# Three moves in the opening of a fused attention and feed-forward kernel: an earlier request for a weight quarter, transposes ahead of table matmuls, one unit swapped in a hand-written order

## The chip, the cores and the metric

The kernel runs on one core of one Trainium2 chip. The metric is the device time of one execution in microseconds (us). Before the change three runs gave 323.81, 324.15 and 324.20 us, a median of 324.15.

The core has a matrix engine (TensorE, PE in the profile, with its weight loads shown as PEld), a vector engine (VectorE, DVE), a scalar engine (ScalarE, ACT), a general engine (GpSimd, POOL), a queue engine (SyncE, SP) and 16 DMA engines. Each compute engine works through its own instructions strictly in order and waits on semaphores for the others. DMA transfers are asked for by SP, ACT or POOL, and run by the 16 DMA engines.

## The reference

Sliding-window attention with a linear position bias per head, followed by a two-layer feed-forward part with a hard-swish between the layers:

```python
batch, n_heads, seq, head_dim = (8, 8, 576, 64)          # q, k, v in float32
scores = scale * q @ k.T;  rel = i - j
scores = where(0 <= rel < 128, scores - slope[h] * rel, -1e9)
attn = softmax(scores);  x = attn @ v                    # x: 4608 tokens x 512
h = x @ w_in                                             # 512 -> 2048
g = h * clip(h + 3, 0, 6) / 6
out = g @ w_out                                          # 2048 -> 512, float32
```

## The kernel before, in words

The order on all five engines is written out by hand: an instruction goes into its engine's stream in the order in which the program calls for it. Only waits on data and on free buffers come on top.

Attention goes by pairs of heads, g = 0 to 31, four pairs to a batch. For the first batch (pairs 0 to 3, `first_batch`, L558) q and k come as runs of nine tokens per partition. `prepare` (L208) casts a run to bf16, `transposes` (L219) turns q and then k with 18 small PE transposes each into a PSUM tile, and a copy (L220) brings each to qT and kT. `tables_diag` (L271) and `tables_off` (L307, L310) put the position bias into a PSUM bank by matmuls with the identity, and `scores_diag` (L296) and `scores_off` (L322, L328) add the score matmuls to it. `exp_full` takes the two exponentials of a pair on ACT (L348, L335), each of a tile of 128x1024. There are two such PSUM banks for scores, so a bank is free again once the exponential before last has read it.

`load_tokens` loads v of a batch as five blocks j of 128 tokens (the last of 64) through SP (L112). `cast_v(b, j, copy)` (L181) casts block j to bf16 into `vbuf`, on DVE (V) or POOL (P). `attend` multiplies the exponentials with v (L383, L391; the matmuls of the last block of queries, qt = 4, come last and are the only ones that read block 4) and divides by the sums on DVE (L412, L413). `back` transposes the result (L432) and copies it to xT (L434, L435, L438).

w_in comes in four quarters of 512 columns, asked for by POOL (`load_w_in`, L166): in `first_batch` the first stands between the casts of v, the second (`second_w_in`, L176) behind a one-element memset that waits for `attend(1)`, the others later. w_out follows in four parts (L171). q and k of the second batch are asked for by SP in `load_double` (L98), behind v; `prepare_double` (L227) casts them on POOL, and `wide_double` (L254) transposes them on PE.

The feed-forward part goes by nine chunks of 512 tokens. For each chunk 16 U units (`moe_up`: four matmuls L451 into a PSUM bank `hps`, then a relu on ACT, L470, and a product on DVE, L471, into `gbuf`) and 16 D units (`moe_down`: four matmuls L501 into a bank `ops`; four D units make 128 rows, then a copy L510 and a store). U units of chunk 1 on share two banks. `fill(n)` puts the next n units into the stream between steps of attention. Chunk 0's 16 U units come first; after that the strings in `ORDER` say how the U units of a chunk alternate with the D units of the chunk before. Their row for chunk 1 is taken in the segment for pairs 8 to 11, where `double` (L242) also transposes k and q with two tiles in turn, with one unit between the two.

In `first_batch`, PE's stream ends with `attend(3)`, `back(2)`, `up_begin(0, 0, 3)` (three of the four matmuls of the first U unit, which need w_in's first quarter and xT of pairs 0 to 2), `back(3)`, `wide_double(1, 0, "q")` and further units.

Of the kernel before, what the change touches and what calls it, by code (L numbers as in the profile page):

```python
# [18 lines left out]
def kernel(  # L19
# [76 lines left out]
    def load_double(b, dp, nm, eng):  # L96
        for e in range(2):
            eng.dma_start(out=ldbuf["qk".index(nm)][:, ds((2 * dp + e) * RT * D, RT * D)],  # L98
                          in_=src_of[nm][b, ds(4 * dp, 4), :, :].rearrange(
                              "(i e) (a t) d -> e a i (t d)", e=2, t=RT)[e])  # L100
# [7 lines left out]
    def load_tokens(b, nm):  # L108
        t = tokens(b, nm)
        for j in range(NQ):  # L110
            n = min(128, S - j * 128)
            nc.sync.dma_start(out=t[:n, j, :, :],  # L112
                              in_=src_of[nm][b, :, ds(j * 128, n), :].rearrange("h p d -> p h d"))
# [36 lines left out]
    def warm_up(n):  # L150
        w = ps_av.tile([128, 128], FP32, tag="av", name="w")
        for _ in range(n):
            nc.tensor.matmul(w, lhsT=ident, rhs=ident, start=True, stop=True)
# [11 lines left out]
    def load_w_in(g):  # L165
        nc.gpsimd.dma_start(  # L166
            out=w_in_sb[:, :, ts(g, 512)],
            in_=moe_w_in[:, ts(g, 512)].rearrange("(k p) f -> p k f", p=128))
# [6 lines left out]
    def second_w_in():  # L175
        nc.gpsimd.memset(w_out_sb[:, 4, 0:1], 0.0)  # L176
        load_w_in(1)

    def cast_v(b, j, copy):
        n = min(128, S - j * 128)  # L180
        copy(out=vbuf[b % 2][:n, j, :, 0:D], in_=ld[b, "v"][:n, j, :, :])  # L181
# [22 lines left out]
    def prepare(g, copies):  # L204
        for nm, copy in zip("qk", copies):
            pr = prs.tile([128, RT * D], BF16, tag=f"pr{nm}", name="pr",
                          padded_shape=[128, 2 * RT * D])
            copy(out=pr, in_=runs[nm][:, g % NP, :])  # L208
            st[g, nm] = pr

    def transposes(g, copies):
        b, hp = divmod(g, NP)
        for nm, dst, copy in (("q", qTb[b % 2], copies[0]), ("k", kTb[b % 2], copies[1])):
            src = st.pop((g, nm))
            tp = ps_h.tile([128, RT, RP], BF16, tag="h", name="tp", padded_shape=[128, 16, 64])
            for t in range(RT):
                for e in range(2):
                    r = slice(e * D, (e + 1) * D)
                    nc.tensor.transpose(tp[r, t, :], src[r, ts(t, D)], ident[r, r])  # L219
            copy(out=dst[:, hp, :, :].rearrange("p j c -> p (j c)")[:, 0:S].rearrange(  # L220
                "p (a t) -> p a t", t=RT), in_=tp.rearrange("p t a -> p a t"))
# [38 lines left out]
    def full(g):  # L260
        return g < NB_FULL * NP
# [4 lines left out]
    def tables_diag(g):  # L266
        scd = ps_sc.tile([128, 2, 512], FP32, tag="sc", name="scd")
        st[g, "scd"] = scd
        for e in range(2 if diag_tabled(g) else 0):
            t = tab[:, 2 * (g % NP) + e, 1:2, :]  # L270
            nc.tensor.matmul(scd[:, e, :].rearrange("p (j c) -> p j c", j=4), lhsT=ident,  # L271
                             rhs=t.to_broadcast([128, 4, 128]), start=True, stop=False)
# [12 lines left out]
    def scores_diag(g):  # L285
        rooms(g)
        b, hp = divmod(g, NP)
        qT, kT = qTb[b % 2][:, hp, :, :], kTb[b % 2][:, hp, :, :]
        first = not diag_tabled(g)
        if (g, "scd") not in st:  # L290
            tables_diag(g)
        scd = st[g, "scd"]
        for j in range(4):
            for e in range(2):
                r = slice(e * D, (e + 1) * D)
                nc.tensor.matmul(scd[:, e, ts(j, 128)], lhsT=kT[r, j, :],  # L296
                                 rhs=qT[r, j, :], start=first, stop=first or j == 3)

    def tables_off(g):
        hp = g % NP  # L300
        sco = ps_sc.tile([128, 2, 512], FP32, tag="sc", name="sco")
        st[g, "sco"] = sco
        if full(g):
            for e in range(2):
                h = 2 * hp + e
                t = tab[:, h, 0:1, :]
                nc.tensor.matmul(sco[:, e, 128:512].rearrange("p (j c) -> p j c", j=3),  # L307
                                 lhsT=ident, rhs=t.to_broadcast([128, 3, 128]),
                                 start=True, stop=False)
                nc.tensor.matmul(sco[:, e, 0:128].rearrange("p (s c) -> p s c", s=2),  # L310
                                 lhsT=ident, rhs=tab[:, h, :, 0:64], start=False, stop=False)

    def scores_off(g):
        b, hp = divmod(g, NP)
        qT, kT = qTb[b % 2][:, hp, :, :], kTb[b % 2][:, hp, :, :]
        foff = not full(g)
        if (g, "sco") not in st:
            tables_off(g)
        sco = st[g, "sco"]
        for e in range(2):  # L320
            r = slice(e * D, (e + 1) * D)
            nc.tensor.matmul(sco[:, e, 64:128], lhsT=kT[r, 4, :],  # L322
                             rhs=qT[r, 4, 0:LAST], start=foff, stop=foff)
        for j in range(4):
            n = 128 if j < 3 else LAST
            for e in range(2):
                r = slice(e * D, (e + 1) * D)
                nc.tensor.matmul(sco[:, e, ds((j + 1) % 4 * 128, n)], lhsT=kT[r, j, :],  # L328
                                 rhs=qT[r, j + 1, 0:n], start=foff, stop=foff or j == 3)
# [8 lines left out]
    def exp_full(g):  # L338
        for e in range(2):
            exp_diag(g, e)  # L340
        exp_off_full(g)
# [113 lines left out]
    def up_begin(nt, ms, n):  # L455
        hps = ps_h.tile([128, NT], FP32, tag="h", name="hps")
        up_mms(nt, ms, 0, n, hps)
        begun[nt, ms] = hps, n
# [29 lines left out]
    def moe_down(nt, step):  # L488
# [14 lines left out]
        if part == 3:  # L503
# [5 lines left out]
            else:  # L509
                nc.vector.tensor_copy(out=osb, in_=ops[nt, sub])  # L510
                nc.sync.dma_start(out=out[rows, :], in_=osb)

    ORDER = [("UUDUDUUDUD", "UUDUDUDUD", "UDUDUDD", "UUDDDD"),
             ("DDDD", "UUDUDUDUD", "UUDUDUDUD", "UUDUDUDDUU"),
             ("DDDD",) * 4]
    units = [(0, moe_up, step) for step in range(16)]
    for nt in range(1, n_nt + 1):
        ups, downs = iter(range(16)), iter(range(16))
        for c in "".join(ORDER[0 if nt == 1 else 2 if nt == n_nt else 1]):
            units.append((nt, moe_up, next(ups)) if c == "U" else (nt, moe_down, next(downs)))  # L520
# [12 lines left out]
    V, P, A = nc.vector.tensor_copy, nc.gpsimd.tensor_copy, nc.scalar.copy  # L533
# [24 lines left out]
    def first_batch():  # L558
        prepare(0, (V, A))
        warm_up(20)  # L560
        tables_diag(0)
        tables_off(0)
        warm_up(10)
        transposes(0, (V, A))
        scores_diag(0)
        prepare(1, (P, V))
        transposes(1, (V, V))
        scores_off(0)
        exp_full(0)
        scores_diag(1)  # L570
        prepare(2, (P, P))
        tables_off(1)
        transposes(2, (V, V))
        scores_off(1)
        exp_full(1)
        scores_diag(2)
        prepare(3, (P, V))
        tables_off(2)
        transposes(3, (V, V))
        scores_off(2)  # L580
        exp_full(2)
        scores_diag(3)
        scores_off(3)
        exp_full(3)
        cast_v(0, 0, V)
        cast_v(0, 1, P)
        load_w_in(0)
        cast_v(0, 2, V)
        cast_v(0, 3, V)
        cast_v(0, 4, P)  # L590
        for dp in range(2):
            for nm in "kq":
                load_double(1, dp, nm, nc.sync)
        load_tokens(1, "v")
        attend(0)
        attend(1)
        back(0)
        attend(2)
        back(1)
        second_w_in()  # L600
        prepare_double(1, 0, (P, P))
        attend(3)
        back(2)
        up_begin(0, 0, 3)
        back(3)
        wide_double(1, 0, "q", V)
        prepare_double(1, 1, (P,), "k")
        load_w_in(2)
        prepare_double(1, 1, (P,), "q")
        load_w_in(3)  # L610
        for dp in range(2):
            for nm in "kq":
                load_double(2, dp, nm, nc.sync)
        up_begin(0, 1, 3)
        done[0] = NP
        fill(1)
        wide_double(1, 0, "k", A)
        fill(2)
# [147 lines left out]
```

## Time and profile before

| what | value |
|---|---|
| runs, us | 323.81, 324.15, 324.20 |
| the profiled execution, its own time, us | 323.38 |
| its span, us | 321.7 |
| instructions | 7010 |
| busy share of the span | PE 96%, ACT 61%, DVE 54%, POOL 44% |
| DMA in the span | 51.90 MB, mean 161 GB/s |
| granted TensorE clock | 1.00 |

The span reaches from the first to the last instruction of the profiled execution. Times inside it count from the span's start. A row of a timeline reads: start, length, engine, line, operation, what it writes and reads, and in square brackets the idle time of its engine just before it and what ended that. A row of the chain of waits reads: start, length, and the work or the wait. A transfer has a row where it is asked for (the queue of the asking engine: SPq, POOLq); the time until it has landed is given with the DMA issues.

### The profile page before, as it was taken

Reading aid. Unit: us, or ns where it says so; the run is one execution under the profiler, and the core shown is the slowest. Engines: PE = TensorE matmul, PEld = TensorE weight load, DVE = VectorE, ACT = ScalarE, POOL = GpSimd, SP = SyncE. Lnnn points to the kernel's source line nnn. Section 1 sums busy time; section 2 is a strip of 40 time slices with the busy share of each in tenths; the row PEclk is TensorE's granted clock in tenths of the full one; section 3 lists DMA queues with packets and bytes.
Section 4 is the critical chain, followed back from the end, with each engine's and each line's share of the span. In section 5 each row is a group of like instructions: output and inputs, shape, how many; then the busy total and the mean of one; then the engine's idle time right before and its main releaser. Section 6 shows DMA issues by size and latency. Waiting matters only on the chain.

```text
span 321.7 us, 7010 instructions
## 1 busy us (share of the span) xinstructions
PE 308.1 (96%) x2699; PEld 166.7 (52%) x2738; DVE 172.7 (54%) x338; ACT 195.1 (61%) x334; POOL 140.7 (44%) x249
## 2 busy tenths in 40 slices
PE   6879999999999999999999999999999999999996
PEld 5465465555555455455677644554554444444443
DVE  6657675554356555555555556555655455455510
ACT  4748976877777766666676657666764344244401
POOL 8456592683494767356745664563331000000000
PEclk9999999999999999999999999999999999999999
DMA  7999999899999999999999999932112200000112
GB/s 277 202 319 225 272 255 208 223 235 204 220 223 184 220 198 201 200 223 205 186 191 191 229 176 201 211 108 86 23 53 64 76 34 35 33 33 33 67 52 79
DMA packets 131425, 51.90 MB, mean 161 GB/s; under 512 B 118976, under 2 KB 123328, under 8 KB 131392
## 3 DMA queue, kind: packets, MB, share of 16 engines
q1 hardware_dynamic: 126160, 45.36, 67.0%
q0 software_dynamic: 4224, 4.19, 8.3%
q10 hardware_dynamic: 1008, 1.90, 1.6%
q8 instruction: 21, 0.34, 0.5%
q14 instruction: 12, 0.10, 0.1%
HBM read 36.70 MB, written 9.44 MB: 143 GB/s over the span
## 4 chain that ended last, share of the span: by engine, by line
PE 82%; DMA 5%; ACT 4%; POOL 4%; issue 2%; DVE 2%; SPq 1%; POOLq 0%
PE ops L501 35%; PE hps L451 35%; DMA ldbuf<-in_q_dram 3%; PE scd L296 2%; DMA qTb<-tbuf 2%; PE av L391 2%; PE av L383 2%; ACT r L470 2%; PE sco L328 1%; PE ops L482 1%; ACT kTb L244 1%; PE tp L254 1%; POOL tbuf L194 1%; ACT gbuf L351 1%; SPq L98 1%
## 5 line engine op out<-in xcount | busy, mean ns | idle before, releaser
L471 DVE SCALAR_TENSOR_TENSOR gbuf<-r,hps 128x512 bf16<-128x512 f32 x144 | 98.7, 687 | 102.5 <-ACT r L470 100.2
L470 ACT ACTIVATE r<-hps,bias 128x512 f32<-128x512 f32 x144 | 98.9, 689 | 89.5 <-PE hps L451 88.2
L451 PE MATMUL hps<-xT,w_in_sb 128*128 128x512 bf16 (+1 forms) x621 | 142.7, 358 | 2.3 <-DMA w_in_sb<-in_moe_w_in_dram 0.9
L501 PE MATMUL ops<-w_out_sb,gbuf 128*128 128x512 bf16 x540 | 134.2, 380 | 2.3 <-issue 1.7
L451 PEld LDWEIGHTS <-w_in_sb 128*128 128x128 bf16 x640 | 58.8, 98 | 54.8 <-DMA w_in_sb<-in_moe_w_in_dram 1.3
L501 PEld LDWEIGHTS <-gbuf 128*128 128x128 bf16 x560 | 52.2, 98 | 57.2
L354 POOL TENSOR_SCALAR_AFFINE_SELECT pd<-pd 128x512 bf16<-128x512 bf16 x48 | 29.6, 631 | 34.5 <-ACT pd L351 34.4
L364 POOL TENSOR_SCALAR_AFFINE_SELECT po<-po 128x512 bf16<-128x512 bf16 x48 | 30.1, 633 | 32.7 <-ACT po L361 32.6
L351 ACT ACTIVATE pd<-scd,bias_d 128x512 bf16<-128x512 f32 x48 | 31.6, 685 | 5.0 <-PE scd L296 3.6
L194 POOL CAST tbuf<-ldbuf 128x512 bf16<-128x512 f32 (+1 forms) x45 | 25.5, 611 | 18.7 <-DMA qTb<-tbuf 9.8
L510 DVE COPY osb<-ops 128x512 f32<-128x512 f32 x33 | 22.7, 687 | 20.3 <-PE ops L501 20.3
L361 ACT ACTIVATE po<-sco,bias_o 128x512 bf16<-128x512 f32 x48 | 33.1, 689 | 0.0
L402 DVE TENSOR_TENSOR avs<-av,rc 128x384 bf16<-128x384 f32 (+1 forms) x48 | 23.6, 491 | 1.6
L391 PEld LDWEIGHTS <-pd 128*128 128x128 bf16 x192 | 14.4, 97 | 8.3 <-issue 0.5
L383 PE MATMUL av<-vbuf,po 128*128 128x65 bf16 x192 | 18.1, 193 | 0.1
L391 PE MATMUL av<-vbuf,pd 128*128 128x65 bf16 x192 | 17.5, 194 | 0.3 <-ACT kTb L244 0.3
L383 PEld LDWEIGHTS <-po 128*128 128x128 bf16 x192 | 14.4, 98 | 3.1 <-DVE avs L402 0.5
L187 POOL CAST vbuf<-ldbuf 128x1024 bf16<-128x1024 f32 x14 | 14.3, 1040 | 3.2 <-DMA ldbuf<-in_v_dram 3.2
L367 ACT ACTIVATE p4buf<-sco,bias_d 128x64 bf16<-128x64 f32 x48 | 15.5, 324 | 0.0
L227 POOL CAST pr<-ldbuf 128x576 bf16<-128x576 f32 x20 | 12.8, 669 | 4.4 <-DMA ldbuf<-in_k_dram 3.4
L296 PE MATMUL scd<-qTb,kTb 64*128 64x128 bf16 x256 | 12.7, 219 | 1.8 <-DVE kTb L220 1.1
L296 PEld LDWEIGHTS <-kTb 64*128 64x128 bf16 x256 | 7.2, 94 | 13.5 <-issue 9.7
(96 smaller groups left out, 215.0 us busy)
## 6 DMA issues: line engine op xcount, KB each, us to landing
out_dram<-osb SPq DMA_DIRECT2D x33, 256.0 KB, 2.4
ldbuf<-in_v_dram SPq DMA_DIRECT2D x32, 256.0 KB, 5.3
ldbuf<-in_q_dram SPq DMA_DIRECT2D x20, 256.0 KB, 5.1
ldbuf<-in_k_dram SPq DMA_DIRECT2D x16, 256.0 KB, 4.6
ldbuf<-in_q_dram SPq DMA_DIRECT2D x12, 288.0 KB, 6.4
ldbuf<-in_k_dram SPq DMA_DIRECT2D x12, 288.0 KB, 6.4
w_in_sb<-in_moe_w_in_dram POOLq DMA_DIRECT2D x4, 512.0 KB, 9.2
w_out_sb<-in_moe_w_out_dram POOLq DMA_DIRECT2D x4, 512.0 KB, 11.1
```

The lines of the kernel that those rows point to most:

```text
L194: nc.gpsimd.tensor_copy(out=tbuf[:m, :, j, :], in_=s[:m, j, :, :].rearrange("p (i e) d -> p i (e d)", e=2))
L296: nc.tensor.matmul(scd[:, e, ts(j, 128)], lhsT=kT[r, j, :], rhs=qT[r, j, :], start=first, stop=first or j == 3)
L351: nc.scalar.activation(out=pd[:, e, :, :].rearrange("p j c -> p (j c)"), in_=sc[:, e, :], func=ACT.Exp, bias=bias_d[:, h:h + 1], scale=scale)
L354: nc.gpsimd.affine_select(out=pd[:, e, :, :], in_=pd[:, e, :, :], pattern=[[0, 4], [1, 128]], channel_multiplier=-1, base=0, compare_op=AL ...
L361: nc.scalar.activation(out=po[:, e, :, :].rearrange("p j c -> p (j c)"), in_=sc[:, e, :], func=ACT.Exp, bias=bias_o[:, h:h + 1], scale=scale)
L364: nc.gpsimd.affine_select(out=po[:, e, :, :], in_=po[:, e, :, :], pattern=[[0, 4], [-1, 128]], channel_multiplier=1, base=-1, compare_op=A ...
L383: nc.tensor.matmul(out_av, lhsT=po[:, e, qt % 4, :], rhs=vb[:, qt - 1, h, :], start=True, stop=False)
L391: nc.tensor.matmul(out_av, lhsT=d, rhs=vb[:, qt, h, :], start=(qt == 0), stop=True)
L451: nc.tensor.matmul(hps[:, lo:hi], lhsT=w_in_sb[:, ks, ts(ms, 128)], rhs=xT[:, ks, ds(src, hi - lo)], start=(ks == 0), stop=(ks == n_ks - 1))
L470: nc.scalar.activation(out=r6, in_=hps, func=ACT.Relu, bias=bias3[:, 0:1], scale=1.0 / 6.0)
L471: nc.vector.scalar_tensor_tensor(out=gts[nt][:, ms, :], in0=r6, scalar=1.0, in1=hps, op0=ALU.min, op1=ALU.mult)
L501: nc.tensor.matmul(ops[nt, sub], lhsT=gts[nt][:, ms, ts(sub, 128)], rhs=w_out_sb[:, ms, :], start=(ms == 0), stop=(ms == n_ms - 1))
```

## The change: what it does

Three edits:

1. In `first_batch`, `transposes` of pairs 2 and 3 stands before `tables_off` of pairs 1 and 2 instead of behind it. The instructions are the same.
2. The first quarter of w_in is asked for behind the cast of v's block 0, which goes to POOL; block 1's cast goes from POOL to DVE. Before, it was asked for behind block 1's cast on POOL.
3. The order of units for chunk 1: the tenth unit becomes a U and the D that stood there comes after it, so that one more U is ahead of chunk 0's later downs; the last row has one U less. There are 16 of each as before.

```diff
-    ORDER = [("UUDUDUUDUD", "UUDUDUDUD", "UDUDUDD", "UUDDDD"),
+    ORDER = [("UUDUDUUDUUD", "UUDUDUDUD", "UDUDUDD", "UDDDD"),
              ("DDDD", "UUDUDUDUD", "UUDUDUDUD", "UUDUDUDDUU"),
              ("DDDD",) * 4]
...
         prepare(2, (P, P))
+        transposes(2, (V, V))
         tables_off(1)
-        transposes(2, (V, V))
         scores_off(1)
         exp_full(1)
         scores_diag(2)
         prepare(3, (P, V))
+        transposes(3, (V, V))
         tables_off(2)
-        transposes(3, (V, V))
         scores_off(2)
         exp_full(2)
         scores_diag(3)
         scores_off(3)
         exp_full(3)
-        cast_v(0, 0, V)
-        cast_v(0, 1, P)
+        cast_v(0, 0, P)
         load_w_in(0)
+        cast_v(0, 1, V)
         cast_v(0, 2, V)
         cast_v(0, 3, V)
         cast_v(0, 4, P)
```

## The prediction

> **What bounds the kernel now.** The page first: TensorE (PE) is the bound, and it is short of work only at the start.
>
> ```profile
> PE 308.1 (96%) x2699; PEld 166.7 (52%) x2738; DVE 172.7 (54%) x338; ACT 195.1 (61%) x334; POOL 140.7 (44%) x249
> PE   6879999999999999999999999999999999999996
> DMA  7999999899999999999999999932112200000112
> ```
>
> Each digit is a slice of 8.04 us. PE is at 6, 8 and 7 tenths in the first three slices, then full until the last. By windows it idles 2.49, 1.10 and 2.21 us in 0:8, 8:16 and 16:24, together 5.8 us, and then some 0.4 us per 8 us. So whatever makes PE's stream start earlier or later near 24 us moves the end one for one, as long as nothing stalls it afterwards. Next the chain of waits in order of time, cut to where PE's idling ends:
>
> ```profile
> 14.50 8.26 DMA ldbuf<-in_q_dram
> 22.76 0.05 issue
> 22.81 0.68 POOL pr L227
> 23.49 0.05 issue
> 23.54 0.68 PE tp L254 x9
> ```
>
> PE starts its full stretch at 23.54, with L254 of the q of batch 1, pairs 0 and 1. That waited for POOL's cast, and the cast for a q load landing at 22.76. A second chain arrives just ahead of it (timelines of PE and POOL):
>
> ```profile
> 16.76 0.23 PE L391 MATMUL wide<-vbuf,w_out_sb 128*128 128x65 bf16 x2 [0.24 <-ACT w_out_sb L348]
> 22.37 0.60 PE L451 MATMUL hps<-xT,w_in_sb 128*128 128x512 bf16 x2 [0.94 <-DMA w_in_sb<-in_moe_w_in_dram]
> 22.80 0.44 PE L432 MATMUL tb<-ident,avs 128*128 128x128 bf16 x5
> ...
> 11.82 0.62 POOL L181 CAST vbuf<-ldbuf 128x512 bf16<-128x512 f32 x1 [1.69 <-DMA ldbuf<-in_v_dram]
> 12.38 0.88 POOL L166 DMA_DIRECT2D w_in_sb<-in_moe_w_in_dram  x1
> 15.80 0.87 POOL L181 CAST vbuf<-ldbuf 64x512 bf16<-64x512 f32 x1 [2.54 <-DMA ldbuf<-in_v_dram]
> 17.97 0.74 POOL L166 DMA_DIRECT2D w_in_sb<-in_moe_w_in_dram  x1
> ```
>
> The reader is to see two things. `attend(0)` starts at 16.76, when the exponentials let it, and v's last block is cast on POOL at 15.80 to 16.67: both release it within 0.1 us. And PE waits 0.94 us for the first w_in quarter, but L254 would wait until 23.54 in any case.
>
> **Part 1, transposes ahead of tables** (pairs 2, 3). Nothing is added; the four table matmuls (9.85 to 10.39, 0.54 us) go behind the 36 transposes. `scores_off` comes no sooner, but DVE's copies start 0.54 earlier (10.91 becomes 10.37), so kT of pair 2 is ready at 11.8 and ScalarE (ACT) loses its gap of 0.28 before 12.83; the same happens for pair 3. ACT's gaps before 12.83, 14.39 and 15.69 are 0.28, 0.54 and 0.28: the gain is between 0 and 1.1. Followed through in order I get 0.8: the last exponential ends near 16.8 instead of 17.63, and `attend(0)` could begin near 15.9. This pays only if v is there.
>
> **Part 2, w_in earlier.** The three v casts that change hands cost nothing: DVE's three casts of 0.42 us and POOL's of 0.62 have idle time around them. What counts is the DMA issue. Block 0 of v was issued at 4.62 and lands some 6.1 us later (the two issues in 4.6:5.05 have a median of 6.4, the second alone 6.7), so near 10.7; POOL has been free since 10.13. Its cast ends at 11.3 and the quarter is asked for at 11.28 instead of 12.38, 1.1 us earlier. In the queue rows its first packets come in 13:14 (3 packets), so they would come near 12.9. Now what is then in the DMA engines:
>
> ```profile
> q8 instruction: 1, 0.02, 4.5%
> ...
> q1 hardware_dynamic: 568, 0.14, 67.6%
> q0 software_dynamic: 3, 0.00, 2.0%
> ...
> q0 software_dynamic: 29, 0.03, 57.3%
> q1 hardware_dynamic: 77, 0.04, 26.4%
> ...
> q0 software_dynamic: 176, 0.18, 106.8%
> q1 hardware_dynamic: 83, 0.02, 16.0%
> ```
>
> (queue: packets, MB, share of 16 engines; windows 10.25:12, 13:14, 14:15 and 34:35.) An instruction fetch held one engine for 4.5% of 16 x 1.75 us, 1.26 us, in the midst of v. So v's packets are nearly all through by 14, and a tail of about 70 small ones trickles on to 15, as slowly as one engine moves them; block 4 lands at 15.8 for that engine's sake. Before, w_in came at 14.0 and needed about 0.9 us to get into stride (29 packets in 14:15 against 176 in a full us), so it missed v. Now it is in stride at 13.8, with 60 to 70 packets of v left on the late engine. The last pair of rows shows what happens when both are there: quarter 3 of w_in beside v of batch 1, where 256 B packets get no more than one turn per 1 KB packet. Those v blocks (issued 28.41 and 29.26) took 9.5 us each to land, those of batch 0 took 5.5 to 7.7.
>
> The price. A quarter is 512 packets, 32 per engine, at 106.8% x 16 / 176 = 0.097 us: 3.1 us. Turn about, the v tail is held by at most that, and by nothing if w_in again comes too late on that engine: 0 to 3.1 us. I take 3.1, because more than 32 packets are left; block 4 lands near 18.9. The Trainium skill, "DMA: Bandwidth & Descriptors", section "Queues, rings and completion order", says that an engine goes round its queues by whole packets of some 9 to 17 descriptors. By that, taking the rows' packets for its descriptors and four of 1 KB to a turn of w_in, 65 small ones would need about five turns of 0.39 us, an estimated 2 us instead of 3.1; the rows of 34:35 speak for one to one.
>
> Behind it: POOL's cast of block 4 (0.61 to 0.87) ends near 19.6, the last four value matmuls of `attend(0)` near 19.9, and its reciprocal starts at 19.8 to 20.0 instead of 17.51, 2.3 late. From there four attends and backs run at their own pace (reciprocals at 17.51, 18.51, 19.68, 20.94), so `back(2)`'s transposes go from 20.99 to 23.3 and xT of pair 2 from 22.11 to 24.4. w_in is then long there (0.94 saved); the three matmuls of `up_begin` and `back(3)` end at 24.9 to 25.0, and L254 goes from 23.54 to about 24.95: **+1.4**. Queued behind v's cast on POOL is also `second_w_in`: asked for near 20.3 instead of 17.97, its packets come near 21.8, against 22 before (q0 falls to 7 packets in 21:22 and stands at 78 in 22:23: the next quarter starts when the one before has landed). So q's last load gets at most 0.4 us of extra turns: it lands at 22.8 to 23.7, its cast ends by 24.4, and it no longer decides. The casts of k for pairs 2 and 3 (25.80 now) may come near 27.1, L254 on them wants 26.52 + 1.4 = 27.9: covered. w_in's second quarter (needed at 28.35 now, landed at 17.97 + 10.4 = 28.4) would land near 28.4 and be needed at 29.8: covered.
>
> **Part 3, the order.** One U moves ahead of the fourth D, and the two kinds alternate one place shifted until the string's last rows. Sixteen of each remain. Loss: the U that now comes at 58.73 needs the bank of the U two before, whose product DVE ends at 58.28 + 0.69 = 58.97: 0.27 late. Gain: in two pairs (before 72.44 and 80.66) a D instead of a U stands between the two transposes of `double`, so ACT's second copy needn't wait behind a relu, and the waits of 0.17 each go. Bounds -0.4 to +0.3; I take **-0.1**. The last part of w_out (issued at 42.9, landing 13.6 us or less later) is wanted 0.86 later than now, which costs nothing.
>
> **Sum.** +1.4 - 0.1 = +1.3. The profiled execution took 323.38 us (span 321.7 and 1.68 around it), so 324.7 for it; it lies 0.77 under the median of the runs, 324.15, to which the forecast is given: **325.4 us**. Its own range, with v's delay between 2 and 3.1 and the extra turns of w_in against q, is 324.9 to 326.2.
>
> **Rivals.**
> Faster: w_in fills the gap. In 14:15 the engines moved only 65 GB/s, against 391 in 19:22; packets brought into that us let k and q land up to 0.8 us earlier, and if v slips by less than 0.5 us, part 1 is worth its 0.8 at the attends. Then L254 starts near 22.7, -0.8, with part 3 -0.9: 323.25. It decides if the late engine has fewer than five packets of v left when w_in is in stride. For it: the idle us and PE's 0.94 wait. Against: the tail of 77 packets, and that q's late packets share an engine that is busy throughout.
> No change: w_in is served on the late engine only behind v, as before. Then quarter 0 and q land there as before, L254 stays at 23.54, and 324.05 follows from part 3 alone. For it: before, the tail of v kept its pace after 14 although w_in had begun elsewhere. Against: 1.1 us more of v are still to come.
> That the change doesn't ask earlier at all would need block 0 to land after 11.8; it is issued 0.4 us before block 1, which landed then, so this gets no chance of its own.
>
> **Chances.** Forecast (slower) 0.55, faster 0.25, no change 0.20. With 0.2% (0.65 us, what a measurement of this kernel can tell): faster 0.25, same 0.20, slower 0.55. The range reaches from the faster case to the top of the forecast's own: 323.1 to 326.2.
>
> **What would show it.** Right: POOL's wait for v's block 4 ends near 18.9 rather than 15.8; PE's `attend(0)` stands split before its last matmuls; L254 starts near 25 and is released by L432 or xT, not by q; w_in's first quarter lands before 19 and no PE wait on it is left. Wrong: block 4 at 15.8 to 16.3 and L254 at or before 23.5. Part 3 is wrong if the two waits of 0.17 stay or if L451 waits more than 0.3 near 59.

## The result, and the profile after

| | runs | median, us | lowest to highest |
|---|---|---|---|
| before, beside the change | 15 | 323.24 | 322.8 to 324.3 |
| the change | 15 | 325.04 | 324.2 to 325.4 |

The ratio of the two is 1.0044, with a 95% interval of 1.0032 to 1.0055: 1.4 us slower, clear of noise and clear of the 0.2% (the two medians lie 1.8 us apart). The profiled execution of the change took 324.83 us (span 323.1), that of before 323.38 (span 321.7): 1.45 us apart. In the wider set of runs the kernel before has a median 0.9 us lower than in the three shown ahead of the prediction.

The page of the change, for the rows shown of before:

```profile
PE 309.9 (96%) x2699; PEld 168.6 (52%) x2738; DVE 172.3 (53%) x338; ACT 194.8 (60%) x334; POOL 140.1 (43%) x249
PE   7879999999999999999999999999999999999996
PEclk9979999999999999999999999999999999999999
```

The loss stays within the opening, and a new thing stands there: the granted TensorE clock falls in the third slice, where before it was at 9 throughout. The chain of waits, in order of time (start, length, what), says what the opening waits for:

```profile
10.23 7.98 DMA ldbuf<-in_v_dram
18.21 0.06 issue
18.27 0.61 POOL vbuf L181
18.89 0.04 issue
18.93 0.19 PE wide L391
...
24.48 0.38 PE hps L451
24.86 0.28 PE tb L432 x5
25.13 0.50 PE tp L254 x9
```

(A row of the chain starts where the work ahead of it ends; in the timeline L254 starts at 24.97.) Before, this chain came to L254 through a load of q. Now it comes through v: the last block, asked for at 10.23, takes 7.98 us to land (5.5 before), and L254 follows on the attends with no wait for q. The timelines of POOL, PE and DVE show the links:

```profile
11.18 0.88 POOL L166 DMA_DIRECT2D w_in_sb<-in_moe_w_in_dram  x1
18.27 0.60 POOL L181 CAST vbuf<-ldbuf 64x512 bf16<-64x512 f32 x1 [6.20 <-DMA ldbuf<-in_v_dram]
...
18.93 0.19 PE L391 MATMUL wide<-vbuf,w_out_sb 128*128 128x65 bf16 x1 [1.66 <-POOL vbuf L181]
...
19.26 0.22 DVE L412 RECIPROCAL rcw<-wide 128x10 f32<-128x10 f32 x1 [3.73 <-PE wide L391]
22.14 0.22 DVE L412 RECIPROCAL rcw<-wide 128x10 f32<-128x10 f32 x1 [0.81 <-PE wide L391]
...
24.97 0.67 PE L254 MATMUL tp<-ident,pr 128*128 128x128 bf16 x9
```

The first and the third reciprocal of before:

```profile
17.51 0.22 DVE L412 RECIPROCAL rcw<-wide 128x10 f32<-128x10 f32 x1 [1.31 <-PE wide L391]
19.68 0.22 DVE L412 RECIPROCAL rcw<-wide 128x10 f32<-128x10 f32 x1
```

w_in is asked for 1.2 us earlier than before (12.38); v's block 4 is cast 2.5 us later (15.80); PE stands still for 1.66 us in the middle of `attend(0)`; DVE's first reciprocal is 1.75 us late (17.51), its third 2.46 us (19.68); L254 starts at 24.97 instead of 23.54, 1.43 us late. The queue rows (packets, MB, share of 16 engines) of the windows 13:14, 14:15 and 15:16 show what holds v:

```profile
q0 software_dynamic: 72, 0.07, 69.4%
q1 hardware_dynamic: 180, 0.04, 26.3%
...
q0 software_dynamic: 179, 0.18, 115.2%
q1 hardware_dynamic: 26, 0.01, 3.8%
...
q0 software_dynamic: 147, 0.15, 88.8%
q1 hardware_dynamic: 123, 0.03, 23.5%
```

In 14:15, where SP's queue was down to 77 packets before, w_in (q0) has 179 packets, as many as in the 34:35 of before (176), and v (q1) has 26. In 15:16 they share, about one for one.

### The profile page after: what moved, and what is told of

It is laid out like the page before. It is cut to its first block, busy times and chain, and to the rows that moved or that the text cites. A ratio compares the mean times of both kernels' runs of the same rounds, so it can differ in the third digit from the quotient of the medians.

```text
span 323.1 us, 7012 instructions
## 1 busy us (share of the span) xinstructions
PE 309.9 (96%) x2699; PEld 168.6 (52%) x2738; DVE 172.3 (53%) x338; ACT 194.8 (60%) x334; POOL 140.1 (43%) x249
## 4 chain that ended last, share of the span: by engine, by line
PE 81%; DMA 6%; ACT 4%; issue 2%; DVE 2%; POOL 2%; SPq 1%; ACTq 0%; POOLq 0%; DVEq 0%
PE ops L501 35%; PE hps L451 35%; DMA ldbuf<-in_v_dram 2%; PE scd L296 2%; DMA qTb<-tbuf 2%; PE av L391 2%; ACT r L470 2%; PE av L383 2%; DMA ldbuf<-in_k_dram 2%; PE sco L328 1%; SPq L112 1%; PE ops L482 1%; PE tb L432 1%; ACT xT L438 1%; DVE gbuf L471 1%
## 5 line engine op out<-in xcount | busy, mean ns | idle before, releaser
L510 DVE COPY osb<-ops 128x512 f32<-128x512 f32 x33 | 22.7, 687 | 22.0 <-PE ops L501 21.9
## 6 DMA issues: line engine op xcount, KB each, us to landing
w_out_sb<-in_moe_w_out_dram POOLq DMA_DIRECT2D x4, 512.0 KB, 12.3
```

## The experiments

Every kernel ran beside the kernel before on the same chip; the ratio is to that.

| kernel | runs | median, us | before, us | ratio, 95% interval |
|---|---|---|---|---|
| part2_alone | 12 | 324.70 | 323.34 | 1.0027, 1.0009 to 1.0045 |
| parts13 | 12 | 324.00 | 323.34 | 1.0013, 0.9999 to 1.0028 |
| part1_alone | 12 | 323.23 | 323.34 | 0.9996, 0.9974 to 1.0018 |
| part3_alone | 12 | 323.65 | 323.34 | 1.0007, 0.9993 to 1.0021 |
| keep_pe_busy | 12 | 324.35 | 323.38 | 1.0024, 1.0009 to 1.0039 |
| casts_only | 12 | 323.26 | 323.38 | 0.9992, 0.9974 to 1.0010 |
| two_quarters | 6 | 327.19 | 323.38 | 1.0097, 1.0070 to 1.0125 |
| try_better | 12 | 322.95 | 323.38 | 0.9983, 0.9967 to 0.9999 |
| block3_last | 10 | 322.65 | 323.39 | 0.9979, 0.9960 to 0.9999 |
| best_of_parts | 12 | 322.75 | 323.39 | 0.9981, 0.9965 to 0.9997 |
| block3_last_earlier | 12 | 323.10 | 323.26 | 0.9984, 0.9963 to 1.0004 |
| best_order | 12 | 323.12 | 323.26 | 0.9984, 0.9963 to 1.0005 |

The medians of any one kernel are blurred by about 1 us that has nothing to do with the opening. In the profile of part1_alone, for one, the stretch from 107 to 125 us is 1.5 us longer than in that of before: POOL waits 6.2 us for a DMA transpose (`qTb<-tbuf`) instead of 4.8, and PE then waits 1.1 us for POOL's masks. So the readings below rest on the place of the steps in the profiles first, and on the medians second.

### Each part alone

**part2_alone**: the kernel before with

```diff
-        cast_v(0, 0, V)
-        cast_v(0, 1, P)
+        cast_v(0, 0, P)
         load_w_in(0)
+        cast_v(0, 1, V)
```

> The kernel before with the w_in request behind block 0's cast, and nothing else. If w_in holding v's block 4 is the cause, this alone costs the whole: block 4 lands near 18.3 instead of 15.8, DVE's first reciprocal of attend starts near 19.3, L254 near 25.0 instead of 23.5, and the time is 1.2 to 1.6 us over before (ratio 1.004 to 1.005). If the order of units or the transposes bring the loss, the ratio is under 1.002.

**parts13**: the change with these lines undone, the rest kept.

> The change without the w_in part. If w_in holding v's block 4 is the cause, block 4 lands near 15.8 again, L254 starts at 23.0 to 23.6 and the time is within 0.4 us of before (ratio 0.999 to 1.001), at best 0.5 faster, since w_in's first quarter and q still land near 22. If the cause is the order of units (its late bank near 59) or the transposes, the ratio stays near 1.004.

**part1_alone** and **part3_alone**: the kernel before with the two `transposes` moved, and with the new first row of `ORDER`.

> Only the transposes ahead of the tables. ACT's last exponential of the first batch ends 0.7 to 0.9 us sooner (near 16.9 instead of 17.6), but v's block 4 (cast until 16.7) and w_in and q (landing near 22 and 22.8) stay, so the time moves by 0 to -0.3 us. Rival: the opening is paced by ACT, then -0.7.

> Only the order of units for chunk 1. My sum had -0.1 us: two waits of 0.17 us of PE on ACT's copy L244 (before 72.4 and 80.7) go, and one wait on DVE's product near 59 to 66 comes. Rival: the waits only move, and the time is the same within 0.1 us, or +0.3 if the bank is late more than once.

POOL's cast of v's last block in part2_alone, and in parts13:

```profile
18.43 0.61 POOL L181 CAST vbuf<-ldbuf 64x512 bf16<-64x512 f32 x1 [6.25 <-DMA ldbuf<-in_v_dram]
```

```profile
15.68 0.61 POOL L181 CAST vbuf<-ldbuf 64x512 bf16<-64x512 f32 x1 [2.40 <-DMA ldbuf<-in_v_dram]
```

With part 2 block 4 is held, without it it is not; L254 starts at 25.57 in part2_alone and at 23.66 in parts13, where POOL's cast of q releases it as before. By the medians part 2 alone is 1.4 us slower, by the ratio 0.3 to 1.5, so this agrees with the whole loss without pinning it; the ratio itself is below the 1.004 that was expected. L254 is 0.6 us later than in the change, and the clock of this profile is at 0.50 for 6.83 us instead of 3.41. Five of its 12 runs kept a clock of 1.00; their median is 323.94, that of the other seven 325.03. parts13 lies 0.4 us above before by the ratio, with an interval from no loss to 0.9 us; in its profile w_in's second quarter came 0.35 us late for the fifth U unit.

How far to trust such places: up to L254 part3_alone has the same instructions as the kernel before, yet its loads land sooner (q at 21.77 instead of 22.76), and L254 starts there so:

```profile
22.83 0.67 PE L254 MATMUL tp<-ident,pr 128*128 128x128 bf16 x9
```

In the four kernels that have the request of before, and its order of steps from `attend(0)` to L254, L254 starts at 22.83 (part3_alone), 22.84 (part1_alone), 23.54 (before) and 23.66 (parts13). Against these the change, at 24.97, is 1.3 to 2.1 us late; the 1.43 is the difference to one profile.

Part 1 gave next to nothing even where it could: ACT's last exponential of the first batch starts at 16.69 in part1_alone and at 16.61 before. Its span from the first to the last exponential shrank by 0.1 us, not by 0.8. The transposes of pair 3 now stand ahead of the tables, so `scores_off(2)` comes later by their length, and ACT waits 1.01 us for it ahead of the exponential at 14.64.

Part 3 took away both waits of 0.17 on L244, as forecast, and brought a wait of 0.18 on DVE's product (at 66.48 in the change, not near 59). Yet between chunk 1's first relu and chunk 2's there are 41.27 us in part3_alone and in the change, and 41.07 before and in part2_alone: 0.2 us lost. Which rows hold it stays open. In part1_alone, which has the old order, the same stretch takes 41.29: there the fourth D unit starts at 58.97 instead of 58.73, when the last part of w_out has landed (58.93; 57.80 before), as in best_order below. So the 0.2 holds against the old order where that does not wait for w_out.

### What the lower clock costs

**keep_pe_busy**: the change, with

```diff
-        av_matmuls(g, range(NQ), lambda qt, e: av[:, e, qt, :])
+        av_matmuls(g, range(NQ - 1), lambda qt, e: av[:, e, qt, :])
+        if g == 0:
+            warm_up(28)
+        av_matmuls(g, (NQ - 1,), lambda qt, e: av[:, e, qt, :])
```

> The changed kernel with 28 dummy matmuls between the value matmuls of attend(0) that need no v block 4 and those that do, so that PE does not idle there. If the lower TensorE clock after that idle us is part of the loss, the granted clock stays at 1.00 in 16:24, the reciprocals of the second and third attend follow each other at the pace of before (1.2 us apart instead of 1.9), L254 starts at 24.2 to 24.5 instead of 25.0, and the time is 0.5 to 0.8 us under the changed kernel's, near 324.4. Rival: the attends are paced by DVE and ACT, the clock does not matter, L254 stays at 25.0.

In the change, the window 19:22 (PE, PEld, DVE, ACT, POOL busy, then granted clock, DMA share, GB/s), and in this kernel 16:24:

```profile
19.00:22.00 3.00, 2.82 (x45) 2.65 (x45) 2.00 (x4) 0.64 (x1) 2.46 (x5) 0.50 1.05 389
```

```profile
16.00:24.00 8.00, 6.65 (x131) 5.58 (x130) 4.09 (x8) 3.54 (x5) 4.67 (x8) 1.00 1.06 340
```

v's block 4 is as late as in the change (cast at 18.21), but PE stays at full clock, and L254 starts at 24.30 instead of 24.97. The median falls by 0.7 us, and the granted clock is 0.999 or more in all 12 runs, against 0.995 or less in 11 of the change's 15. The change's own runs say the same: these 11 have a median of 325.14, the four at 0.998 or more one of 324.5. So about half of the loss is v's lateness, and about half is PE's slower clock behind the stall. The Trainium skill, "TensorE: Matmul & The Clock Gate", Part 1, puts the clock's window at 3.4 us, and a return to half rate after at least one such window of idling. The 3.4 us at half rate agree (the trace has the clock at 0.50 for 3.41 us), the idling does not: here it was one wait of 1.66 us, and 1.80 us of idling in all in the 3.41 us before the clock fell.

### The time of the request, or who casts

**casts_only**: the casts as in the change, the request delayed until block 1 has landed:

```diff
         cast_v(0, 0, P)
+        nc.gpsimd.tensor_copy(out=warm, in_=ld[0, "v"][:, 1, 0, 0:1])
         load_w_in(0)
         cast_v(0, 1, V)
```

> The changed kernel, casts dealt out as in the change (block 0 on POOL, block 1 on DVE), but POOL reads one column of block 1 before it asks for w_in, so that the request falls near 12.3 as before. If the time of the request is the cause, v's block 4 lands near 15.8 and the kernel is as fast as the one without the w_in part (ratio 1.000 to 1.002). If dealing out the casts costs, it stays at 1.004.

The request falls at 11.71, half a us later than in the change, and block 4 is cast at 15.81 as before. The queue rows of 13:14 and 14:15:

```profile
q1 hardware_dynamic: 539, 0.13, 64.9%
q0 software_dynamic: 18, 0.02, 36.4%
...
q0 software_dynamic: 101, 0.10, 85.9%
q1 hardware_dynamic: 50, 0.01, 8.5%
```

v has 539 packets in 13:14, where the change has 180; w_in comes behind it and then has the engines to itself. Its quarter lands 6.9 us after the request instead of 9.7 before, and L254 starts at 22.76, 0.8 us sooner than in the profile of before, but only 0.1 sooner than in part3_alone and part1_alone; with a ratio of 0.9992 (0.9974 to 1.0010) a gain is not shown. So who casts costs nothing, and half a us in the request decides whether block 4 is held.

**two_quarters**: the change with `load_w_in(1)` right behind `load_w_in(0)`, and the second one taken out of `second_w_in`.

> The changed kernel with the second w_in quarter asked for right behind the first, behind block 0's cast: twice the suspected cost. If w_in packets hold whatever v is still out, v's block 4 lands near 21 (3 us more), L254 near 27.5 to 28 and the time is 2.5 to 3 us over the changed kernel. Rival: the second request only gets its first packets some 4 us after it was made, behind block 4; then block 4 stays at 18.3, q is 1 to 2 us later and the time is 0.5 to 1.5 us over the changed kernel.

Its ratio is 1.0097 against the change's 1.0044, so 0.5% or 1.7 us over the change (2.15 by the medians, 327.19 and 325.04): it lies between the two expectations and settles neither. Of the 16 engines' landings of block 4, 15 came at 17.3 to 18.2 as in the change and one at 19.89; block 4 got through largely between the two quarters, whose packets begin at 12.90 and 16.76. L254 starts at 26.66, and q landed at 24.0.

**block3_last** asks for v's blocks in another order: `for j in (0, 1, 4, 2, 3)`, the rest as in the change. **block3_last_earlier** asks for w_in ahead of block 0's cast besides.

> The changed kernel, but SP asks for v's blocks in the order 0, 1, 4, 2, 3. If w_in holds whatever v block is asked for last, block 4 is cast early (before 14.5) and block 3 is held instead: DVE's cast of it ends near 18.5, attend(0) stands split before the matmuls of its fourth and fifth query block, L254 starts near 25 and the time is that of the changed kernel within 0.5 us. Rival: what is slow is block 4 itself, with 64 partitions and its cast on POOL; then nothing is held and the time is near before's.

> As block3_last, but w_in is asked for as soon as block 0 has landed, ahead of its cast: near 10.75 instead of 11.24. If w_in's first packets follow the request (1.6 us in the changed kernel), they come near 12.4, before the packets of the last block (3) get going near 13, and block 3 is put off behind w_in as block 4 was: it lands after 17, L254 near 25, 1 us or more over block3_last. Rival: in block3_last w_in's packets were held up by v's own (first at 13.56, 2.3 us after the request), and they come near 13.5 again: then nothing changes, within 0.3 us.

POOL's request and its cast of block 4 in block3_last:

```profile
11.24 0.88 POOL L166 DMA_DIRECT2D w_in_sb<-in_moe_w_in_dram  x1
13.91 0.60 POOL L181 CAST vbuf<-ldbuf 64x512 bf16<-64x512 f32 x1 [1.78 <-DMA ldbuf<-in_v_dram]
```

My theory of "whatever comes last is held" fell: with the same request (11.24) nothing was held, and the kernel was 0.2% faster than before. The trace of packets suggests why. In the order 0 to 4 v's packets have a lull at 12.8 to 13.2, ahead of block 4, for which SP issues until 12.2. w_in asked for at 11.2 finds it: its first packets come at 12.82, and those of block 4 then begin near 15.0 instead of 13.3. Asked for at 11.7, its first packets come at 13.47, behind the start of block 4. In block3_last SP has issued the last block by 10.8, and v has no lull there: its packets keep 211 to 222 per quarter us from 12.3 to 13.5, w_in's first come at 13.50, and in block3_last_earlier, asked for 0.5 us sooner, at 13.54, so that its rival came true. So w_in's packets seem to come in when v's leave room, and a block that has not begun by then is put off. These four kernels fit this; part1_alone does not: there w_in's first packets came 2.6 us after the request, at 15.37, though all but a trickle of v (about 7 packets per tenth of a us) was through by 14.1. So the start of w_in's packets is not fully explained, and why a begun stream of w_in puts off the start of the next block by 1.7 us is open. The rival in its plain form, that block 4 itself is slow, is not excluded either: with block 4 third, it is also SP's issue of the last block that gets shorter (0.89 us for block 3, 2.0 for block 4).

### Versions that beat both

**try_better** leaves w_in where it was, and puts `up_begin(0, 1, 3)` ahead of `wide_double(1, 0, "q")` and the second quarter's request behind `attend(0)`, with part 1. **best_of_parts** is casts_only without part 3; **best_order** is block3_last without part 3.

> The kernel before with the transposes ahead of the tables, the first matmuls of the second U unit ahead of L254, so that PE starts without q, and the second w_in quarter asked for behind attend(0) instead of attend(1). w_in's first quarter stays where it was. If PE's start is bound by w_in's first quarter (near 22) once q is taken off the path, the first relu of chunk 0 moves up by 0.4 to 0.8 us and the time is 0.3 to 0.7 us under before (ratio 0.998 to 0.999). Rival: w_in's second quarter, landing near 28.4, takes the place of q as the last wait, and the time is that of before.

> The kernel before with the transposes ahead of the tables and w_in asked for the moment block 1 has landed (near 11.7, as in casts_only), block 0 cast on POOL and block 1 on DVE; the order of units as before. Block 4 lands near 15.8, w_in's first quarter before 19, L254 starts at 22.7 to 22.9 and the first relu of chunk 0 near 24.4 instead of 25.2, so the time is 0.5 to 0.8 us under before (ratio 0.9975 to 0.9985). Rival: at 11.7 the request is at the edge, and in part of the runs it holds block 4 after all; then the runs fall in two groups 1 us or more apart, and the median is not under before's.

> block3_last with the order of units as before, that is the transposes ahead of the tables, w_in asked for behind block 0's cast, and v's block 4 asked for ahead of blocks 2 and 3. Part 3 seemed to cost 0.2 us in the profiles that have it. So 322.3 to 322.6, ratio 0.997 to 0.998; rival: part 3 is worth nothing either way and this equals block3_last within 0.1 us.

Five kernels come out 0.2% under before, three with intervals that end just below 1 (block3_last 0.9979, best_of_parts 0.9981, try_better 0.9983). best_of_parts did what was expected of it (L254 at 22.79). In try_better the rival half came true: L254 for k of pairs 2 and 3 waits 1.1 us; that the second quarter's packets hold that load is likely, but not tested. best_order has the earliest chunk 1 (1.09 us ahead of the profile of before at its first relu, 0.7 ahead of part3_alone), and gives 0.9 of it back ahead of chunk 2, most of it here (who waits for what: us in total, times, longest):

```profile
PE ops L501 <- DMA w_out_sb<-in_moe_w_out_dram: 0.7, 1, 0.7
```

The fourth D unit comes too soon for the last part of w_out. block3_last_earlier, which has part 3, opens as early (1.08) and keeps 0.88. Between these two profiles part 3 saves 0.7 us; between casts_only (41.27) and best_of_parts (41.42) it saves 0.15. So part 3 costs 0.2 us where the last part of w_out has landed in time and saves that wait where it has not; it belongs with an earlier opening, and the change did not bring one. In the times this does not show: best_order was expected at 0.997 to 0.998 and came out at 0.9984, level with block3_last_earlier.

## Why the prediction was right

- **The result**: forecast +1.3 us, measured +1.4 by the ratio and +1.8 by the medians. The forecast of 325.4 us started from 324.15, 0.9 above the median of the wider set; the change has a median of 325.04.
- **v's block 4**: forecast to land near 18.9, measured 18.2. That w_in's packets hold it is shown by part2_alone, parts13 and casts_only. The picture was too narrow: I had only the one late engine hold v by turns, 3.1 us. In fact block 4 lands late on all 16 engines (16.9 to 18.2), because its packets begin 1.7 us later; the turns of one for one come after that (123 of v beside 147 of w_in in 15:16). So the cause was right, and its size was right only in part for the reason given.
- **The attends**: forecast 2.3 us late at the first reciprocal, measured 1.75; then the clock took 0.7 more by the third, which I did not have. The two errors cancel: L254 was forecast near 24.95 and starts at 24.97. So the sum was right to 0.1 us, but one of its terms was too big by 0.55, and one of about 0.7 was missing. That it came out so close is luck, the more so as with the old request L254 lies anywhere from 22.83 to 23.66.
- **q**: rightly off the path. But its reason was partly wrong: w_in's second quarter was to start when the first has landed. Its first packets came 3.9 us after its request, as before, though the first quarter had landed 1.6 us ahead of that request.
- **Part 1**: forecast 0.8 us on the last exponential, hidden behind v; measured 0.1. It cost the sum nothing, since it was hidden.
- **Part 3**: forecast -0.1, measured +0.2 against the profile of before, and level with part1_alone (41.27 and 41.29). The two waits went; the one that came was 0.18 instead of 0.27; where the rest goes is unexplained. The prediction saw that the last part of w_out is wanted 0.86 us later and put that at nothing; it is a gain wherever the fourth D unit of the old order has to wait for it, as in part1_alone, best_of_parts and best_order.
- **The faster rival**: casts_only has its signs, block 4 on time and L254 at 22.76, where I had 22.7. It needs the request half a us later than the change makes it. But two kernels with the old request start L254 at 22.83 and 22.84, and the time of casts_only is that of before, so its gain is not shown.

## What to carry to other kernels

A request for a large transfer that nobody waits for yet can still cost: look at what is being landed in the 2 us behind the request, and whether some of it has not begun. A move of half a us decided here whether the last block of v was cast at 15.8 or at 18.3. Before a step's start is compared between two profiles, look how far it moves between profiles of kernels that are the same up to it; here that was 0.7 us, half of the loss. When a stall is added to a matrix engine that has run at full clock, count the slower clock behind it as well.

## What the runs showed of the hardware

- A PE wait of 1.66 us was enough, in the profile of the change, for 3.41 us at a granted clock of 0.50; 11 of its 15 runs show a lowered clock (0.995 or less), four do not (0.998 or more). With dummy matmuls in the wait the clock stayed at 1.00.
- In all 14 profiles the clock rises and falls only at whole multiples of 3.41 us from its first rise. Ahead of the kernel's end it fell behind stretches of 3.41 us on this grid in which PE was idle for 1.43 us (part2_alone), 1.80 (the change) and 3.06 (two_quarters), and stayed up behind all with 1.23 or less. At the kernel's end it stayed up behind 1.60 (casts_only) and 1.70 (part2_alone), so idle time alone does not decide. How a wait lies on this grid may decide whether it costs the clock; that would fit the four runs of the change that kept it, but is not tested.
- The second request on POOL's queue got its first packets 3.4 to 4.2 us after it was made in 13 kernels (before: asked for at 18.0, first packet at 22.0; the change: 19.4 and 23.3), whether or not the first quarter had landed; in two_quarters it took 4.6. The first request got its packets after 1.6 to 2.8 us.
- Packets of POOL's queue stayed out while the other queue's ran without a gap: 2.3 us after the request in block3_last and 2.8 us in block3_last_earlier, against 1.6 in the change.
